# Softmax sums of the last four segments dealt one to each PE column tile, first memory queries put ahead of the others

## The chip, the cores and the metric

The kernel runs on one core of one Trainium2 chip. The metric is the time of one execution in device microseconds.

## The reference, cut to what matters

Four layers run one after the other: an FFT layer A, an attention layer B, A again, B again. Layer B cuts 2048 rows into 64 segments of 32. Each segment attends to 8 memory rows and to itself, for 32 heads of 128:

```python
for s in range(n_seg):
    h = jnp.concatenate([mem, xs], axis=1)            # 8 memory rows, 32 rows
    ...
    scores = jnp.where(mask, q @ k * scale, -1e9)
    p = _softmax(scores, axis=-1)                     # sum over keys, then divide
    o = p @ v ... Wo
    mem = o[:, :M, :]                                 # memory of the next segment
```

The kernel does all segments of a head at once. It works with one memory query per segment; only the first segment keeps the seven others, since its memory rows differ. These seven are "the first memory queries" (`PRE = 7`). A head thus has 64 x 33 + 7 = 2119 queries, in five groups: four of 15 segments and one of the last 4.

## The kernel before: the parts that matter

Keys lie on partitions in 17 tiles of 128. For every tile and group, the queries that see keys of that tile form a run of columns, and each run is one matmul in three stages: scores, sums, values. The layout puts the seven queries last, so they fall into the fifth group although their keys are in tile 0:

```python
    PRE = MEM - 1; SW = SEG + 1; GS = 15; NG = 5; NT = 17
    QPRE = NSEG * SW                   # the 7 first memory queries come last
    GQ = GS * SW                       # 495 columns per group
    def qbase(self, s):
        return self.SW * s
    # ... self.tiles[t] = [(group, lo, hi, offset in P), ...]
```

The sums are matmuls with a block of ones, 32 output rows wide. Four groups go to the four column tiles of the PE array (rows 0 to 31, 32 to 63 and so on of one PSUM buffer) and run side by side. The fifth goes to rows 0 to 31 of the last scores' buffer, that is to column tile 0, where the first group already is:

```python
def sums(h, P, ps_last):
    psl = pa.tile([128, 512], FP32, name="psl", tag="psl", bufs=1)
    ps4 = ps_last[0:32, 512 - NL:512]
    for i in range(max(len(r) for r in runs)):
        for g_ in range(NG):
            # ...
            dst = psl[32 * g_:32 * g_ + 32, :] if g_ < 4 else ps4
            nc.tensor.matmul(dst[:, lo - q0:hi - q0], lhsT=ones[:, 0:32], rhs=P[:, off:off + hi - lo], ...)
    # ... five ACT copies into sums_sb: 4 groups side by side, then 139 columns of the fifth
def sums_ln(h):    # Ln on ACT, sum into an accumulator on POOL
def sums_back(h):  # Exp(-x) on ACT = 1/sum, two stores to DRAM, one broadcast load to all partitions
def value_group(h, P, Rb, oT, g_):
    # matmuls of V with P into pso, then DVE multiplies pso by the reciprocals
```

All engines but POOL follow one manual order. In the pass of head h, keys, queries and values of h are computed, with scores and sums of h - 1 and values of h - 2 put in between:

```python
post = [lambda: sums(...), lambda: sums_ln(h - 1), lambda: sums_back(h - 1)]
merge(dense, parts + [g1[0], post[0], g1[1], post[1], g1[2], post[2], g1[3], g1[4]])
```

Of the kernel before, what the change touches and what calls it, by code (L numbers as in the profile page):

```python
# [691 lines left out]
class _Stream:  # L692
# [11 lines left out]
    NT = 17  # L704
    NK = NT * 128
    NQ = PRE + NSEG * SW
    QPRE = NSEG * SW
    GQ = GS * SW
    NM = PRE + NSEG
    NC = PRE + NSEG - 1  # L710
    NX = NSEG * SEG
# [3 lines left out]
    def __init__(self):  # L715
        PRE, SW, GS = self.PRE, self.SW, self.GS
        kseg = np.full(self.NK, -1)
        kpos = np.zeros(self.NK, dtype=int)
        kw = np.zeros(self.NK)
        kseg[0:PRE], kpos[0:PRE], kw[0:PRE] = 0, np.arange(PRE), 1  # L720
        for s in range(NSEG):
            b = self.kbase(s)
            rows = np.arange(b, b + SW)
            if s == NSEG - 1:
                rows[SW - self.TAIL:] = self.TAILK + np.arange(self.TAIL)
            kseg[rows] = s
            kpos[rows] = np.concatenate([[MEM - 1], MEM + np.arange(SEG)])
            kw[rows] = 1
            kw[b] = 1 if s == 0 else MEM
        qseg = np.zeros(self.NQ, dtype=int)  # L730
        qpos = np.zeros(self.NQ, dtype=int)
        qpos[self.QPRE:] = np.arange(PRE)
        for s in range(NSEG):
            b = self.qbase(s)
            qseg[b:b + SW] = s
            qpos[b:b + SW] = np.concatenate([MEM + np.arange(SEG), [MEM - 1]])
        self.hgap = [(self.hcol(a), self.hcol(b)) for a, b in ((502, 512), (1007, 1024), (1519, 1536), (2035, 2048))]
        self.q0 = [0] + [self.qbase(g * GS) for g in range(1, self.NG)] + [self.NQ]
        ok = (kseg[:, None] == qseg[None, :]) & ((qpos[None, :] < MEM) | (qpos[None, :] >= kpos[:, None]))
        full = np.where(ok, kw[:, None], 0.0)  # L740
        self.tiles = []
        cols = []
        off = 0
        for t in range(self.NT):
            blk = full[t * 128:(t + 1) * 128]
            used = np.flatnonzero(blk.any(axis=0))
            runs = []
            for g in range(self.NG):
                u = used[(used >= self.q0[g]) & (used < self.q0[g + 1])]
                if len(u):  # L750
                    lo, hi = int(u[0]), int(u[-1]) + 1
                    runs.append((g, lo, hi, off))
                    cols.append(blk[:, lo:hi])
                    off += hi - lo
            self.tiles.append(runs)
        self.NP = off
        self.mask = np.concatenate(cols, axis=1).astype(np.float32)
        self.parts = [[t] if t == self.NT - 1 else [t, t + 1] for t in range(0, self.NT, 2)]
        for p in self.parts:
            assert sum(hi - lo for t in p for _, lo, hi, _ in self.tiles[t]) <= 512  # L760
# [3 lines left out]
        return 512 * g + (self.PRE if g == 0 else 0) + self.SW * i  # L764

    def qbase(self, s):
        return self.SW * s

    def hcol(self, k):

# [268 lines left out]
def _b_fast_pass(tc, g, bs, env, flag_col, nxt=None):  # L1039
# [2 lines left out]
    hT, gq, oTm = bs.hT, bs.gq, bs.oTm  # L1042
    ones = g["ones"]
    oTx_d = g["oTx_d"]
    PRE, SW, GS, NG, NT, NQ, QPRE = st.PRE, st.SW, st.GS, st.NG, st.NT, st.NQ, st.QPRE
    scale = float(DH) ** -0.5
    Wd = {n: g[n].rearrange("(c p) h e -> p c (h e)", p=128) for n in ("Wq", "Wk", "Wv")}
    kruns = [(0, 502), (512, 1007), (1024, 1519), (1536, 2035), (2048, 2176)]
# [3 lines left out]
    pa = octx.enter_context(tc.tile_pool(name="b_pa", bufs=2, space=PSUM))  # L1052
    last = {}
    ar = env["ar"]
    GQ, NL = st.GQ, NQ - st.GQ * (NG - 1)
    HPRE, HL = H - 4, H - 2
    s6 = bs.s6
    s3, s4, s5 = (ar.get(s, f"b{bs.lname}") for s in ("S3", "S4", "S5"))
    Vs = [s3.bf(NT, 256) for _ in range(2)]
    s3.o = SLOT["S3"] - 4 * (GQ + NL)  # L1060
    accR, accS = s3.f32(GQ + NL), s3.f32(GQ + NL)
    wts = [{n: s6.bf(5, 256) for n in ("Wq", "Wk", "Wv")} for _ in range(2)]
    oTs = [s6.bf(st.NX) for _ in range(2)]
    QTs = [s4.bf(NQ + 1) for _ in range(2)]
    KTs = [s4.bf(st.NK) for _ in range(2)]
    Ps = [s5.bf(st.NP) for _ in range(2)]
    Es = [s5.bf(512) for _ in range(2)]
    Rb1, sums_sb = s5.f32(NQ), s5.f32(GQ + NL)
    Rs = [s4.f32(GQ + NL), g["R"][:]]
    if True:  # L1070
        nc.gpsimd.memset(sums_sb[:, GQ:], 1.0)
        for KT in KTs:
            for a, b in ((502, 512), (1007, 1024), (1519, 1536), (2035, 2048)):
                nc.gpsimd.memset(KT[:, a:b], 0.0)
# [40 lines left out]
        def q_m(w, h):  # L1115
            QT = QTs[h % 2]
            ps = pj.tile([128, 512], FP32, name="psq", tag="pj")
            chain(w["Wq"], h % 2, ps[:, 0:PRE], hT, 0, PRE)
            chain(w["Wq"], h % 2, ps[:, PRE:st.NM], gq, 0, NSEG)
            nc.scalar.mul(out=QT[:, QPRE:NQ], in_=ps[:, 0:PRE], mul=scale)  # L1120
            nc.scalar.mul(out=x_view(QT, 0, NSEG)[:, :, SEG], in_=ps[:, PRE:st.NM], mul=scale)

        def q_run(w, h, g_):
            QT = QTs[h % 2]
            lo, hi = kruns[g_]
            ps = pj.tile([128, 512], FP32, name="psq", tag="pj")
            chain(w["Wq"], h % 2, ps[:, 0:hi - lo], hT, lo, hi)
            n = GS if g_ < NG - 1 else 3
            o = st.kbase(g_ * GS) - lo
            qv = x_view(QT, st.qbase(g_ * GS), n)  # L1130
            nc.scalar.mul(out=qv[:, :, 0:SEG], in_=x_view(ps, o, n)[:, :, 1:SW], mul=scale)  # L1131
            if g_ < NG - 1:
                nc.scalar.mul(out=qv[:, :, SEG], in_=x_view(ps, o, n)[:, :, 0], mul=scale)
            if g_ == 0:
                nc.scalar.mul(out=QT[:, QPRE:NQ], in_=ps[:, 0:PRE], mul=scale)
            elif g_ == NG - 2:
                q_tail(QT, ps, SEG - st.TAIL, st.TAILK - lo, st.TAIL)
            elif g_ == NG - 1:
                nc.scalar.mul(out=x_view(QT, st.qbase(NSEG - 4), 4)[:, :, SEG], in_=ps[:, 0:3 * SW + 1:SW], mul=scale)
                q_tail(QT, ps, 0, 3 * SW + 1, SEG - st.TAIL)  # L1140
# [30 lines left out]

        def sums(h, P, ps_last):
            psl = pa.tile([128, 512], FP32, name="psl", tag="psl", bufs=1)
            ps4 = ps_last[0:32, 512 - NL:512]
            for i in range(max(len(r) for r in runs)):
                for g_ in range(NG):
                    if i >= len(runs[g_]):
                        continue
                    t, (_, lo, hi, off) = runs[g_][i]
                    dst = psl[32 * g_:32 * g_ + 32, :] if g_ < 4 else ps4  # L1180
                    nc.tensor.matmul(dst[:, lo - st.q0[g_]:hi - st.q0[g_]], lhsT=ones[:, 0:32], rhs=P[:, off:off + hi - lo],  # L1181
                                     start=(i == 0), stop=(i == len(runs[g_]) - 1), skip_group_check=True)
            for dst, src, ns in ((sums_sb[:, 0:GQ], psl, GS), (sums_sb[0:32, GQ:GQ + NL], ps4, NSEG - (NG - 1) * GS)):
                v, nx = x_view(src, 0, ns), ns * SEG
                nc.scalar.copy(out=dst[:, 0:nx].rearrange("p (r s j) -> p r s j", r=16, j=2), in_=byclass(v))
                nc.scalar.copy(out=dst[:, nx:nx + ns], in_=v[:, :, SEG])
            nc.scalar.copy(out=sums_sb[0:32, GQ + QPRE - 4 * GQ:GQ + NL], in_=ps4[:, QPRE - 4 * GQ:NL])  # L1187

        def sums_ln(h):
            nc.scalar.activation(out=Rs[h % 2], in_=sums_sb, func=ACTF.Ln, bias=g["floor"][:, 0:1])  # L1190
# [13 lines left out]
        def sums_back(h):  # L1204
            R = Rs[h % 2]
            nc.scalar.activation(out=R, in_=R, func=ACTF.Exp, scale=-1.0)
            if h == H - 1:
                return
            Rd = g["dram"].tile([1, NQ], FP32, name="Rd", tag="Rd", bufs=3)
            nc.sync.dma_start(out=Rd[0:1, 0:4 * GQ].rearrange("o (g n) -> (o g) n", g=4), in_=R[0:128:32, 0:GQ])  # L1210
            nc.sync.dma_start(out=Rd[0:1, 4 * GQ:NQ], in_=R[0:1, GQ:GQ + NL])
            nc.sync.dma_start(out=Rbs2[h % 2], in_=Rd[0:1, :].to_broadcast([128, NQ]))

        def sums_wide(P, Rb, g_):
            q0, n = st.q0[g_], st.q0[g_ + 1] - st.q0[g_]
# [7 lines left out]
        def value_group(h, P, Rb, oT, g_):  # L1223
# [4 lines left out]
                nc.tensor.matmul(pso[:, lo - q0:hi - q0], lhsT=V[:, t, (h % 2) * 128:(h % 2 + 1) * 128], rhs=P[:, off:off + hi - lo],  # L1228
                                 start=(i == 0), stop=(i == len(runs[g_]) - 1), skip_group_check=True)
            s0, ns = g_ * GS, min(GS, NSEG - g_ * GS)  # L1230
            po, nx = x_view(pso, 0, ns), ns * SEG
            if h < H - 1:
                rx, rm = Rb[:, q0:q0 + nx].rearrange("p (r s j) -> p r s j", r=16, j=2), Rb[:, q0 + nx:q0 + nx + ns]
            else:
                rq = x_view(Rb, q0, ns)
                rx, rm = byclass(rq), rq[:, :, SEG]
            nc.vector.tensor_tensor(out=oT.rearrange("p (r s j) -> p r s j", r=16, j=2)[:, :, s0:s0 + ns, :], in0=byclass(po), in1=rx, op=ALU.mult)  # L1237
            nc.vector.tensor_tensor(out=oTm[:, h, PRE + s0:PRE + s0 + ns], in0=po[:, :, SEG], in1=rm, op=ALU.mult)  # L1238
            if g_ < NG - 1:
                return  # L1240
            nc.vector.tensor_tensor(out=oTm[:, h, 0:PRE], in0=pso[:, QPRE - q0:n], in1=Rb[:, QPRE:NQ], op=ALU.mult)

        def store(h, oT):
            if h < HL:
# [39 lines left out]
        if True:  # L1284
            for h in range(H + 2):
# [7 lines left out]
                if h == 0:  # L1293
# [2 lines left out]
                    q_x(w, 1)  # L1296
                    s1 = ar.get("S1", f"b{bs.lname}")
                    oT0 = s1.bf(HL, 512)
                    Rbs2 = [s1.f32(NQ), Rb1]
                dense, parts, groups = [], [], []  # L1300
                if h < H:
                    def both(run):
# [51 lines left out]
    with octx:  # L1354
# [3 lines left out]
                          lambda c: [(PRE, st.NC, gq[:, c, 1:NSEG]), (0, PRE, gq[:, c, 1:2].to_broadcast([128, PRE]))], st.NM, st.NC)  # L1358
        xns = None
        if nxt is not None:  # L1360
            s3.o = SLOT["S3"] - 4 * (GQ + NL)
            xns = [s3.bf(D) for _ in range(3)]
            nxt.x = x
            nxt.begin_stage1(T)

# [218 lines left out]
def make_globals(ctx, tc, Wq, Wk, Wv, Wo, mem0):  # L1584
# [20 lines left out]
    g["st"] = st = _Stream()  # L1605
    g["gq"] = sp.tile([128, 5, NSEG], BF16, name="gqf")
    g["oTm"] = sp.tile([128, H, st.NM + 1], BF16, name="oTmf")
    g["R"] = sp.tile([128, st.GQ + st.NQ - st.GQ * (st.NG - 1)], FP32, name="R")
    g["m0"] = sp.tile([MEM, D], BF16, name="m0")
    g["u"] = sp.tile([128, 5, NSEG], BF16, name="u")  # L1610
    g["mask"] = sp.tile([128, st.NP], BF16, name="maskf")
# [110 lines left out]
```

## Time and profile before

| | before |
|---|---|
| median of 4 runs | 1580.68 us (1579.67 to 1581.49) |
| span of the profiled run | 1577.2 us |
| PE, ACT, DVE, POOL busy | 1541.9, 834.3, 783.7, 279.3 us |
| one block of sums, first start to what follows | 457 ns, x64 |
| stage B1, B2 (see below) | 667.44, 662.52 us |

The span, from the first instruction to the last, is some 2 us shorter than the time of the same run (1577.2 and 1579.07 us here). A "stage" is measured between two matmul starts in the trace: B1 from the first key matmul of layer 1's attention to the first transform matmul (line 424) of the FFT layer after it, B2 from the first key matmul of the second attention layer to the last matmul of the kernel. The lines that carry the bound are shown in the prediction. The page's rows of matmuls give the time that one spends in the pipe (165 to 375 ns each); what one costs is the distance to the next start.

### The profile page before, as it was taken

The page shows a single profiled execution, that of the slowest core. Times are in us where ns is not written, and L with a number is a line of the kernel's source. Part 1 is how long each engine was busy: PE and PEld are TensorE (multiplying, and loading weights), DVE is VectorE, ACT ScalarE, POOL GpSimd, SP SyncE. Part 2 cuts the span into 40 slices and gives each one's busy share as a digit, 9 for nine tenths or more (in the row PEclk, how much of TensorE's full clock was granted, in tenths as well). Part 3 has the DMA queues.
Part 4 walks back from the last instruction along what each step waited for, and adds up shares of the span by engine and source line. Part 5 has one row for each costly group of instructions (what it writes and reads, how often), then busy time and mean ns, then how long its engine had stood idle before and what let it go on. Part 6 is the DMA issues. An engine that isn't in the chain of part 4 may idle for free. (4 is left out here: it accounts for less than half of the span.)

```text
span 1577.2 us, 36639 instructions
## 1 busy us (share of the span) xinstructions
PE 1541.9 (98%) x14420; PEld 1073.3 (68%) x14421; DVE 783.7 (50%) x2198; ACT 834.3 (53%) x2549; POOL 279.3 (18%) x327
## 2 busy tenths in 40 slices
PE   6999999999999999999999999999999999999998
PEld 5676676666766666677766766666766666677775
DVE  7872545454554545533377545454555545543101
ACT  4584666666666666511126656666666666663000
POOL 3620121111212111100034111111212111120000
PEclk9999999999999999999999999999999999999999
DMA  4680545445454453745114515445454454437242
GB/s 170 213 305 6 153 129 141 130 121 175 122 149 122 134 163 104 216 103 172 51 55 148 182 54 143 128 122 175 124 147 122 136 160 130 142 97 227 68 130 62
DMA packets 159890, 214.13 MB, mean 136 GB/s; under 512 B 7198, under 2 KB 133468, under 8 KB 151772
## 3 DMA queue, kind: packets, MB, share of 16 engines
q1 hardware_dynamic: 159132, 209.41, 44.8%
q8 instruction: 114, 1.87, 0.5%
q0 software_dynamic: 576, 2.30, 0.4%
q14 instruction: 68, 0.56, 0.1%
HBM read 166.59 MB, written 45.09 MB: 134 GB/s over the span
## 5 line engine op out<-in xcount | busy, mean ns | idle before, releaser
L1087 PEld LDWEIGHTS <-bB_S 128*128 128x128 bf16 x3180 | 258.0, 97 | 174.7 <-issue 1.1
L1237 DVE TENSOR_TENSOR bB_S<-pso,bB_S 128x480 bf16<-128x480 f32 (+1 forms) x320 | 189.4, 592 | 246.7 <-PE pso L1228 235.6
L1166 ACT ACTIVATE bB_S<-pss 128x269 bf16<-128x269 f32 (+5 forms) x576 | 203.9, 386 | 199.1 <-PE pss L1163 194.0
L1393 PE MATMUL psx<-Wo_sb,bB_S 128*128 128x320 bf16 x2048 | 287.7, 299 | 0.0
L1146 DVE CAST bB_S<-psk 128x495 bf16<-128x495 f32 (+3 forms) x320 | 191.6, 599 | 114.2 <-PE psk L1087 75.8
L1393 PEld LDWEIGHTS <-bB_S 128*128 128x128 bf16 x2048 | 197.1, 98 | 74.3 <-DVE bB_S L1237 0.7
L1167 DVE TENSOR_TENSOR bB_S<-bB_S,maskf 128x269 bf16<-128x269 bf16 (+5 forms) x576 | 159.3, 288 | 162.1 <-ACT bB_S L1166 162.1
L1192 POOL TENSOR_TENSOR bB_S<-bB_S,bB_S 128x634 f32<-128x634 f32 x62 | 95.1, 1533 | 682.1 <-ACT bB_S L1187 682.1
L1155 ACT CAST bB_S<-psv 128x512 bf16<-128x512 f32 (+1 forms) x288 | 161.2, 560 | 75.7 <-PE psv L1153 75.1
L1131 ACT ACTIVATE bB_S<-psq 128x96 bf16<-128x96 f32 x300 | 152.3, 508 | 91.2 <-PE psq L1087 90.3
L1153 PE MATMUL psv<-bB_S,B2hT_S 128*128 128x256 bf16 x1360 | 166.2, 273 | 0.0
L1153 PE MATMUL psv<-bB_S,B1hT_S 128*128 128x256 bf16 x1360 | 166.2, 273 | 0.0
L1087 PE MATMUL psk<-B1hT_S,bB_S 128*128 128x495 bf16 (+3 forms) x800 | 162.4, 343 | 0.4 <-ACT bB_S L1108 0.2
L1087 PE MATMUL psk<-B2hT_S,bB_S 128*128 128x495 bf16 (+3 forms) x800 | 162.4, 343 | 0.3 <-ACT bB_S L1108 0.2
L1163 PEld LDWEIGHTS <-bB_S 128*128 128x128 bf16 x1216 | 99.6, 97 | 84.4
L1087 PE MATMUL psq<-B2hT_S,bB_S 128*128 128x495 bf16 (+5 forms) x780 | 153.2, 336 | 0.0
L1087 PE MATMUL psq<-B1hT_S,bB_S 128*128 128x495 bf16 (+5 forms) x780 | 153.2, 336 | 0.0
L1153 PEld LDWEIGHTS <-B1hT_S 128*128 128x128 bf16 x1360 | 127.5, 98 | 14.6 <-issue 0.2
L1153 PEld LDWEIGHTS <-B2hT_S 128*128 128x128 bf16 x1360 | 127.5, 98 | 14.6 <-issue 0.2
L1163 PE MATMUL pss<-bB_S 128*128 128x132 bf16 (+8 forms) x1216 | 133.0, 215 | 0.1
L1228 PE MATMUL pso<-bB_S,bB_S 128*128 128x132 bf16 (+8 forms) x1216 | 120.2, 216 | 1.6 <-DVE oTmf L1238 1.4
L1228 PEld LDWEIGHTS <-bB_S 128*128 128x128 bf16 x1216 | 90.6, 98 | 22.8 <-DVE oTmf L1238 4.0
(282 smaller groups left out, 1539.4 us busy)
## 6 DMA issues: line engine op xcount, KB each, us to landing
bB_S<-Rd SPq DMA_DIRECT2D x62, 1059.5 KB
oTx_d<-bB_S SPq DMA_DIRECT2D x60, 512.0 KB
bB_S<-oTx_d SPq DMA_DIRECT2D x46, 512.0 KB
bB_S<-in_B_Wq_dram SPq DMA_DIRECT2D x32, 320.0 KB
bB_S<-in_B_Wk_dram SPq DMA_DIRECT2D x32, 320.0 KB
bB_S<-in_B_Wv_dram SPq DMA_DIRECT2D x32, 320.0 KB
Wo_sb<-in_B_Wo_dram SPq DMA_DIRECT2D x4, 1280.0 KB
B1wv_S<-in_B_Wv_dram SPq DMA_DIRECT2D x10, 512.0 KB
```

The costliest lines, as they stand in the source:

```text
L1087: nc.tensor.matmul(ps, lhsT=w[:, ch, hh * 128:(hh + 1) * 128], rhs=src[:, ch, lo:hi], start=(ch == 0), stop=(ch == 4))
L1131: nc.scalar.mul(out=qv[:, :, 0:SEG], in_=x_view(ps, o, n)[:, :, 1:SW], mul=scale)
L1146: nc.vector.tensor_copy(out=KTs[h % 2][:, lo:hi], in_=ps[:, 0:hi - lo])
L1153: nc.tensor.matmul(ps[:, i * 256:(i + 1) * 256], lhsT=hT[:, ch, st.hcol((t + i) * 128):st.hcol((t + i) * 128) + 128], rhs=w["Wv"][:, ch, : ...
L1155: nc.scalar.copy(out=V[:, t:t + n, :].rearrange("p a b -> p (a b)"), in_=ps[:, 0:n * 256])
L1163: nc.tensor.matmul(ps[:, off - o0:off - o0 + hi - lo], lhsT=KT[:, t * 128:(t + 1) * 128], rhs=QT[:, lo:hi], start=True, stop=True)
L1166: nc.scalar.activation(out=E[:, 0:n], in_=ps[:, 0:n], func=ACTF.Exp)
L1167: nc.vector.tensor_tensor(out=P[:, o0:o0 + n], in0=E[:, 0:n], in1=bs.mask[:, o0:o0 + n], op=ALU.mult)
L1192: nc.gpsimd.tensor_tensor(out=accS, in0=accS, in1=sums_sb, op=ALU.add)
L1228: nc.tensor.matmul(pso[:, lo - q0:hi - q0], lhsT=V[:, t, (h % 2) * 128:(h % 2 + 1) * 128], rhs=P[:, off:off + hi - lo], start=(i == 0), st ...
L1237: nc.vector.tensor_tensor(out=oT.rearrange("p (r s j) -> p r s j", r=16, j=2)[:, :, s0:s0 + ns, :], in0=byclass(po), in1=rx, op=ALU.mult)
L1393: self.tc.nc.tensor.matmul(ps[:, 0:320], lhsT=lhs(h, k // 2), rhs=self.g["Wo_sb"][:, h, c0:c0 + 320], start=(h == 0), stop=(h == H - 1))
```

## The change

The intent: take three small matmuls per head away (the seven queries join tile 0's first run in scores, values and sums), and give the fifth group's sums to all four column tiles, 33 columns each, rather than to the one that has most already. The rows of sums become 535 columns wide and not 634, so Ln, Exp, the accumulators and the stores get shorter, and one of two stores goes. The next layer's norm rows move from the buffer that also holds the accumulators to another. The core of the diff, with cuts marked:

```diff
-    QPRE = NSEG * SW
+    NR = GQ + SW + PRE
...
     def qbase(self, s):
-        return self.SW * s
+        return self.PRE + self.SW * s
...
         def sums(h, P, ps_last):
-            ps4 = ps_last[0:32, 512 - NL:512]
-            for i in range(max(len(r) for r in runs)):
-                for g_ in range(NG):
-                    dst = psl[32 * g_:32 * g_ + 32, :] if g_ < 4 else ps4
...
+            for i in range(max(len(r) for r in runs[:-1])):
+                for g_ in range(NG - 1):
+                    ...  # as before, into psl on tile g_
+            top = ps_last[:, 512 - SW:512]
+            for g_ in range(NG - 1):
+                jobs.append((g_, top, off + SW * g_, True, g_ < NG - 2))
+            jobs.append((NG - 2, top[:, SW - (tail[2] - tail[1]):SW], tail[3], False, True))
...
-            nc.sync.dma_start(out=Rd[0:1, 0:4 * GQ].rearrange(...), in_=R[0:128:32, 0:GQ])
-            nc.sync.dma_start(out=Rd[0:1, 4 * GQ:NQ], in_=R[0:1, GQ:GQ + NL])
+            nc.sync.dma_start(out=Rd[0:1, :].rearrange("o (g n) -> (o g) n", g=4), in_=R[0:128:32, :])
...
-            s3.o = SLOT["S3"] - 4 * (GQ + NL)
-            xns = [s3.bf(D) for _ in range(3)]
+            xns = [s1.bf(D) for _ in range(3)]
```

The last job is a run of 5 columns: the last segment has four keys in tile 15, so its sums need one more matmul, on tile 3.

More of the change, by code (lines that the diff above doesn't have):

```diff
@@ L731, in __init__ @@
         qpos = np.zeros(self.NQ, dtype=int)
-        qpos[self.QPRE:] = np.arange(PRE)
+        qpos[0:PRE] = np.arange(PRE)
         for s in range(NSEG):
@@ L1044, in _b_fast_pass @@
     oTx_d = g["oTx_d"]
-    PRE, SW, GS, NG, NT, NQ, QPRE = st.PRE, st.SW, st.GS, st.NG, st.NT, st.NQ, st.QPRE
+    PRE, SW, GS, NG, NT, NQ, NR = st.PRE, st.SW, st.GS, st.NG, st.NT, st.NQ, st.NR
     scale = float(DH) ** -0.5
@@ L1054, in _b_fast_pass @@
     ar = env["ar"]
-    GQ, NL = st.GQ, NQ - st.GQ * (NG - 1)
     HPRE, HL = H - 4, H - 2
@@ L1059, in _b_fast_pass @@
     Vs = [s3.bf(NT, 256) for _ in range(2)]
-    s3.o = SLOT["S3"] - 4 * (GQ + NL)
-    accR, accS = s3.f32(GQ + NL), s3.f32(GQ + NL)
+    s3.o = SLOT["S3"] - 4 * NR
+    accR, accS = s3.f32(NR), s3.f32(NR)
     wts = [{n: s6.bf(5, 256) for n in ("Wq", "Wk", "Wv")} for _ in range(2)]
@@ L1067, in _b_fast_pass @@
     Es = [s5.bf(512) for _ in range(2)]
-    Rb1, sums_sb = s5.f32(NQ), s5.f32(GQ + NL)
-    Rs = [s4.f32(GQ + NL), g["R"][:]]
+    Rb1, sums_sb = s5.f32(4 * NR), s5.f32(NR)
+    Rs = [s4.f32(NR), g["R"][:]]
     if True:
-        nc.gpsimd.memset(sums_sb[:, GQ:], 1.0)
+        nc.gpsimd.memset(sums_sb[:, GS * SW + SW:], 1.0)
         for KT in KTs:
@@ L1119, in q_m @@
             chain(w["Wq"], h % 2, ps[:, PRE:st.NM], gq, 0, NSEG)
-            nc.scalar.mul(out=QT[:, QPRE:NQ], in_=ps[:, 0:PRE], mul=scale)
-            nc.scalar.mul(out=x_view(QT, 0, NSEG)[:, :, SEG], in_=ps[:, PRE:st.NM], mul=scale)
+            nc.scalar.mul(out=QT[:, 0:PRE], in_=ps[:, 0:PRE], mul=scale)
+            nc.scalar.mul(out=x_view(QT, PRE, NSEG)[:, :, SEG], in_=ps[:, PRE:st.NM], mul=scale)
         def q_run(w, h, g_):
@@ L1134, in q_run @@
             if g_ == 0:
-                nc.scalar.mul(out=QT[:, QPRE:NQ], in_=ps[:, 0:PRE], mul=scale)
+                nc.scalar.mul(out=QT[:, 0:PRE], in_=ps[:, 0:PRE], mul=scale)
             elif g_ == NG - 2:
@@ L1173, in sums @@
             psl = pa.tile([128, 512], FP32, name="psl", tag="psl", bufs=1)
-            ps4 = ps_last[0:32, 512 - NL:512]
-            for i in range(max(len(r) for r in runs)):
-                for g_ in range(NG):
-                    if i >= len(runs[g_]):
-                        continue
-                    t, (_, lo, hi, off) = runs[g_][i]
-                    dst = psl[32 * g_:32 * g_ + 32, :] if g_ < 4 else ps4
-                    nc.tensor.matmul(dst[:, lo - st.q0[g_]:hi - st.q0[g_]], lhsT=ones[:, 0:32], rhs=P[:, off:off + hi - lo],
-                                     start=(i == 0), stop=(i == len(runs[g_]) - 1), skip_group_check=True)
@@ L1183, in sums @@
-            for dst, src, ns in ((sums_sb[:, 0:GQ], psl, GS), (sums_sb[0:32, GQ:GQ + NL], ps4, NSEG - (NG - 1) * GS)):
-                v, nx = x_view(src, 0, ns), ns * SEG
-                nc.scalar.copy(out=dst[:, 0:nx].rearrange("p (r s j) -> p r s j", r=16, j=2), in_=byclass(v))
-                nc.scalar.copy(out=dst[:, nx:nx + ns], in_=v[:, :, SEG])
-            nc.scalar.copy(out=sums_sb[0:32, GQ + QPRE - 4 * GQ:GQ + NL], in_=ps4[:, QPRE - 4 * GQ:NL])
+            jobs = []
+            for i in range(max(len(r) for r in runs[:-1])):
+                for g_ in range(NG - 1):
+                    t, (_, lo, hi, off) = runs[g_][i]
+                    b = lo - st.q0[g_] + (PRE if g_ else 0)
+                    jobs.append((g_, psl[:, b:b + hi - lo], off, i == 0, i == len(runs[g_]) - 1))
@@ new lines, in sums @@
+            tail, (_, lo, hi, off) = runs[-1][0][1], runs[-1][1][1]
+            top = ps_last[:, 512 - SW:512]
+            for g_ in range(NG - 1):
+                jobs.append((g_, top, off + SW * g_, True, g_ < NG - 2))
+            jobs.append((NG - 2, top[:, SW - (tail[2] - tail[1]):SW], tail[3], False, True))
+            for g_, dst, off, first_, last_ in jobs:
+                nc.tensor.matmul(dst[32 * g_:32 * g_ + 32, :], lhsT=ones[:, 0:32], rhs=P[:, off:off + dst.shape[1]], start=first_, stop=last_,
+                                 skip_group_check=True)
@@ L1189, in sums_ln @@
+            v, nx = x_view(psl, PRE, GS), GS * SEG
+            nc.scalar.copy(out=sums_sb[:, 0:nx].rearrange("p (r s j) -> p r s j", r=16, j=2), in_=byclass(v))
+            nc.scalar.copy(out=sums_sb[:, nx:nx + GS], in_=v[:, :, SEG])
+            nc.scalar.copy(out=sums_sb[0:32, NR - PRE:NR], in_=psl[0:32, 0:PRE])
+            nc.scalar.copy(out=sums_sb[:, NR - PRE - SW:NR - PRE], in_=top)
         def sums_ln(h):
@@ L1208, in sums_back @@
                 return
-            Rd = g["dram"].tile([1, NQ], FP32, name="Rd", tag="Rd", bufs=3)
-            nc.sync.dma_start(out=Rd[0:1, 0:4 * GQ].rearrange("o (g n) -> (o g) n", g=4), in_=R[0:128:32, 0:GQ])
-            nc.sync.dma_start(out=Rd[0:1, 4 * GQ:NQ], in_=R[0:1, GQ:GQ + NL])
-            nc.sync.dma_start(out=Rbs2[h % 2], in_=Rd[0:1, :].to_broadcast([128, NQ]))
+            Rd = g["dram"].tile([1, 4 * NR], FP32, name="Rd", tag="Rd", bufs=3)
+            nc.sync.dma_start(out=Rd[0:1, :].rearrange("o (g n) -> (o g) n", g=4), in_=R[0:128:32, :])
+            nc.sync.dma_start(out=Rbs2[h % 2], in_=Rd[0:1, :].to_broadcast([128, 4 * NR]))
         def sums_wide(P, Rb, g_):
@@ L1230, in value_group @@
             s0, ns = g_ * GS, min(GS, NSEG - g_ * GS)
-            po, nx = x_view(pso, 0, ns), ns * SEG
-            if h < H - 1:
-                rx, rm = Rb[:, q0:q0 + nx].rearrange("p (r s j) -> p r s j", r=16, j=2), Rb[:, q0 + nx:q0 + nx + ns]
+            o, nx = PRE if g_ == 0 else 0, GS * SEG
+            po = x_view(pso, o, ns)
+            if h == H - 1:
+                rq = x_view(Rb, q0 + o, ns)
+                rx, rm, rp = byclass(rq), rq[:, :, SEG], Rb[:, 0:PRE]
+            elif g_ < NG - 1:
+                r = Rb[:, NR * g_:NR * g_ + NR]
+                rx, rm, rp = r[:, 0:nx].rearrange("p (r s j) -> p r s j", r=16, j=2), r[:, nx:nx + GS], r[:, NR - PRE:NR]
             else:
-                rq = x_view(Rb, q0, ns)
+                rq = Rb.rearrange("p (s n) -> p s n", n=NR)[:, :, NR - PRE - SW:NR - PRE]
                 rx, rm = byclass(rq), rq[:, :, SEG]
@@ L1238, in value_group @@
             nc.vector.tensor_tensor(out=oTm[:, h, PRE + s0:PRE + s0 + ns], in0=po[:, :, SEG], in1=rm, op=ALU.mult)
-            if g_ < NG - 1:
-                return
-            nc.vector.tensor_tensor(out=oTm[:, h, 0:PRE], in0=pso[:, QPRE - q0:n], in1=Rb[:, QPRE:NQ], op=ALU.mult)
+            if g_ == 0:
+                nc.vector.tensor_tensor(out=oTm[:, h, 0:PRE], in0=pso[:, 0:PRE], in1=rp, op=ALU.mult)
         def store(h, oT):
@@ L1298, in _b_fast_pass @@
                     oT0 = s1.bf(HL, 512)
-                    Rbs2 = [s1.f32(NQ), Rb1]
+                    Rbs2 = [s1.f32(4 * NR), Rb1]
                 dense, parts, groups = [], [], []
@@ L1360, in _b_fast_pass @@
         if nxt is not None:
-            s3.o = SLOT["S3"] - 4 * (GQ + NL)
-            xns = [s3.bf(D) for _ in range(3)]
+            xns = [s1.bf(D) for _ in range(3)]
             nxt.x = x
@@ L1607, in make_globals @@
     g["oTm"] = sp.tile([128, H, st.NM + 1], BF16, name="oTmf")
-    g["R"] = sp.tile([128, st.GQ + st.NQ - st.GQ * (st.NG - 1)], FP32, name="R")
+    g["R"] = sp.tile([128, st.NR], FP32, name="R")
     g["m0"] = sp.tile([MEM, D], BF16, name="m0")
```

## The prediction

> **What bounds the kernel now.** I read four views of the kernel before, in this order: the page's busy table, the chain of waits that ended last, PE's own waits, and the timeline of PE in windows of under a microsecond. The busy table:
>
> ```profile
> PE 1541.9 (98%) x14420; PEld 1073.3 (68%) x14421; DVE 783.7 (50%) x2198; ACT 834.3 (53%) x2549; POOL 279.3 (18%) x327
> ...
> PEclk9999999999999999999999999999999999999999
> ```
>
> PE is near full and always at full clock, the others are at half. A busy PE row does not prove much, because matmuls overlap, so I asked who is waited for. The chain runs nearly everywhere from one matmul to the next:
>
> ```profile
> PE psv L1153 9%; PE psk L1087 9%; PE psx L1393 9%; PE psq L1087 9%; PE pso L1228 2%; PE pss L1163 2%; PE psl L1181 1%; PE psq L1106 1%; PE psm L863 0%; PE psvb L1486 0%; PE psg L1554 0%; DMA Rd<-bB_S 0%; PE pss L1181 0%; ACT bB_S L1108 0%; PE psw L1218 0%
> ```
>
> and PE's waits in the part that the change touches (lines 1163, 1181, 1228) come to 1.4 us in all:
>
> ```profile
> PE ps L324 <- DVE A1xn_S L315: 10.0, 1, 10.0
> PE pso L1228 <- DVE oTmf L1238: 1.4, 4, 0.5
> ```
>
> In the windows 150 to 650 us and 924 to 1430 us (the two attention stages) PE is busy 499.83 of 500.00 and 505.18 of 506.00 us. So the kernel is a queue of matmuls. The time changes by what the change takes from PE's issue order, and hardly by anything else.
>
> The mean of a matmul row (170 ns for 7 columns) is how long one is in the pipe, not what it costs. The cost is the distance from its start to the next start. Three narrow windows of the timeline give it:
>
> ```profile
> 400.66 0.43 PE L1163 MATMUL pss<-bB_S 128*128 128x132 bf16 x5
> 400.92 0.37 PE L1087 MATMUL psk<-B1hT_S,bB_S 128*128 128x495 bf16 x1
> ```
>
> ```profile
> 414.70 0.27 PE L1228 MATMUL pso<-bB_S,bB_S 128*128 128x7 bf16 x3
> 414.81 0.66 PE L1087 MATMUL psk<-B1hT_S,bB_S 128*128 128x128 bf16 x6
> ```
>
> ```profile
> 408.98 0.80 PE L1087 MATMUL psq<-B1hT_S,bB_S 128*128 128x499 bf16 x3
> 409.71 0.24 PE L1181 MATMUL psl<-bB_S,ones 128*32 128x132 bf16 x4
> 409.77 0.17 PE L1181 MATMUL pss<-bB_S,ones 128*32 128x7 bf16 x1
> 409.78 0.30 PE L1181 MATMUL psl<-bB_S,ones 128*32 128x137 bf16 x7
> 409.87 0.17 PE L1181 MATMUL pss<-bB_S,ones 128*32 128x5 bf16 x1
> 409.89 0.24 PE L1181 MATMUL psl<-bB_S,ones 128*32 128x148 bf16 x4
> 409.96 0.22 PE L1181 MATMUL pss<-bB_S,ones 128*32 128x132 bf16 x1
> 410.01 0.22 PE L1181 MATMUL psl<-bB_S,ones 128*32 128x119 bf16 x1
> 410.16 0.36 PE L1228 MATMUL pso<-bB_S,bB_S 128*128 128x132 bf16 x3
> ```
>
> The first shows five score matmuls (132, 7, 144, 148, 119 columns) in 0.26 us. The second shows the last value group (7, 5, 132 columns) in 0.11 us. The third shows one block of sums: 19 matmuls of 32 output rows each, 0.45 us from the first to what follows it, with four of them starting within 10 ns and so running side by side. From the start times of all 64 occurrences in the trace I take medians: 7 columns cost 28 ns in the score stage and 28 in the value stage, 5 columns 25 to 27, 132 columns 57 to 58, 144 columns 62, 148 columns 63. One block of sums takes 457 ns (455 to 460 in all 64).
>
> **What the Trainium skill says.** TensorE: Matmul & The Clock Gate, Back-to-back issue gap, gives an isolated gap of N/2.4 + 2.5 ns and a floor of about 25 ns for up to 64 columns. The trace agrees: 132 columns at 57 to 58 ns (formula 57.5), 7 columns at 28 ns. So a 7-column matmul nearly costs the floor, and widening a neighbour by 7 columns costs 7/2.4 = 3 ns. TensorEngine Tiling (Array Packing), Key Properties, says that tiles run independently and that "Mode switching requires drain". The trace agrees with both: the four starts 3 ns apart, and around a block of sums the gap is 97 ns longer than the columns before it going in, 99 ns coming out. The same page, PSUM Bottleneck, warns that PSUM eviction may become the limit; here ACT, which evicts the sums, is 53% busy and PE waits for it nowhere in these stages.
>
> **The change part by part.** There are 32 heads in each of two layers, so each per-head item counts 64 times. The order of instructions in the changed kernel, set against the old, confirms the counts.
>
> 1. Scores. The seven memory queries now lie ahead of segment 0, so tile 0 is one matmul of 139 columns in place of 132 and 7. Removed 28 ns, added 3 ns: 25 ns x 64 = **1.6 us**, all on PE's path.
> 2. Values. The 7-column matmul of the last group joins the first matmul of the first group in the same way: 25 ns x 64 = **1.6 us**.
> 3. Sums. In the old block, column tile 0 had to do the first group and the whole last group: 132, 7, 144, 5, 148, 132, 119 columns, starting at 0, 68, 98, 160, 186, 250 and 308 ns. Then 50 ns of columns and 99 ns of leaving make 457. The other three tiles had their last start at 199 to 208 ns and sat idle. The new block deals the 132 columns out as 33 to each tile: tile 0 does 139, 144, 148, 119, 33; tile 3, now the longest, does 132, 137, 141, 112, 33, 5. From the old starts of tile 3 (10, 78, 142, 208) its 33 should start near 260 (112 columns cost 51), its 5 near 289 (33 columns cost the floor, 27 to 29), and the block should end between 289 + 99 = 388 and 289 + 25 + 99 = 413. I take 400: 57 ns x 64 = **3.6 us**. Two matmuls are added per block, which cancels the two removed in 1 and 2, so the count stays the same to within two; the gain is in where they run.
> 4. Off the path. ACT copies per block go from five (581 + 215 + 263 + 163 + 169 ns) to four: the 263 and the 163 go, one of 128x33 comes at some 230 (estimate, from the 215 of 15 columns): 0.2 us. Ln and Exp fall from 634 to 535 columns, some 0.1 us each by their own slope (estimate, 828 x 99/634 is the upper bound, 0.13). So ACT falls by some 0.4 us x 64 = 25 us of 834. POOL's adds fall from 1533 ns to about 1533 x 535/634 = 1294, that is 124 x 0.24 = 30 us. One of two small stores per head goes (62), and the broadcast that follows grows by 1% (2140 columns for 2119). DVE has the same 2198 instructions, with the 7-column multiply (156 ns) moved from the last group to the first. All this is hidden, since PE does not wait for it: worth 0.
> 5. The next layer's norm rows in another buffer. In the hand-over after layer 1 (650 to 740 us) PE is busy 89.22 of 90 us, so nothing is there to win: 0.
>
> Sum: 1.6 + 1.6 + 3.6 = 6.8 us, and 1580.4 - 6.8 = 1573.6 us, or 0.4%.
>
> **The rivals.** (a) The sums gain nothing, because the block is held by the drain or by loading the ones into the array (21 loads in place of 19), not by tile 0's queue. For it: 196 of the 457 + 97 ns around a block are drain. Against it: tile 0's starts follow its columns one by one. Then only 3.2 us come: 1577. (b) The whole block shortens further, because all four tiles' queues are better filled and the start lag of 7 to 35 ns between rounds goes. If the block took the bare columns (583 on tile 0, 243 ns) plus 99, it would gain 115 ns x 64 = 7.4 us, together 10.6: 1570. (c) A new wait. The sums of the last four segments now need all 128 rows of the last scores' buffer, one DVE operation of 156 ns is added to the first value group, and each layer's end has DVE behind: there PE waits 0.65 and 0.40 us. That could cost 0.3 us per layer, not more. (d) Start addresses of the queries shift by 7 columns, so odd and even change places. Matmuls of 132 to 148 columns cost 1 to 7 ns over their columns, without a pattern that I could tie to the address; if there is one, 34 matmuls per head x 64 x 1 ns = 2.2 us either way. (e) The single store of 4x535 delays the broadcast. Its wait now touches PE once, for 0.3 us, at each layer's start.
>
> **Range and chances.** The centre is 1573.6. Rival (a) and a loss from (d) give 1577 to 1579, rival (b) with a gain from (d) gives 1568. Runs of the old kernel spread by 1.3 us. I choose 1569 to 1578. A gain over 2% would need 31 us, four times what lies on these three lines; a loss of 2% would need a wait that no view hints at.
>
> **What would show it.** Right: the 7-column rows of lines 1163 and 1228 gone, and 139-column ones spaced near 60 ns; a block of sums near 400 ns from first start to what follows; entry and exit gaps still 97 and 99; ACT near 809 and POOL near 249 us busy, the span unmoved by them; PE still over 499 of 500 us busy in the attention windows. Wrong: a block of sums at 450 or at 340; a new line in PE's waits that names ACT, DVE or the store; or all score and value matmuls slower by a few ns each.

## More of the kernel before

Runs of one kernel scatter by 1 to 3 us, so where a difference is smaller than that I read it from start times in the trace and not from the clock. There is one trace of each kernel.

## The result, and the profile after

The changed kernel takes 1571.99 us (median of 4 runs, 1571.49 to 1573.32) against 1580.68. The ratio is 0.9947, with a 95% interval of 0.9929 to 0.9964. The same kernel once more, in a later job (the run e10_again), gave 1572.91 us and 0.9950 (0.9936 to 0.9964). All outputs are right.

The busy table of the kernel after, in the same columns as before (busy us, share of the span, instructions):

```profile
PE 1536.3 (98%) x14418; PEld 1072.5 (68%) x14419; DVE 787.4 (50%) x2198; ACT 818.5 (52%) x2485; POOL 228.5 (15%) x327
```

PE has two instructions fewer and is as full as before: still the bound. The three narrow windows of its timeline that answer to those in the prediction (start us, length us, engine, line, operation, count) are, for scores:

```profile
399.30 0.41 PE L1162 MATMUL pss<-bB_S 128*128 128x139 bf16 x4
399.54 1.00 PE L1086 MATMUL psk<-B1hT_S,bB_S 128*128 128x495 bf16 x4
```

for the last value group:

```profile
413.25 0.25 PE L1231 MATMUL pso<-bB_S,bB_S 128*128 128x5 bf16 x2
413.34 0.87 PE L1086 MATMUL psk<-B1hT_S,bB_S 128*128 128x128 bf16 x7
```

and for one block of sums:

```profile
408.33 0.42 PE L1185 MATMUL psl<-bB_S,ones 128*32 128x139 bf16 x16
408.58 0.20 PE L1185 MATMUL pss<-bB_S,ones 128*32 128x33 bf16 x5
408.72 0.41 PE L1231 MATMUL pso<-bB_S,bB_S 128*128 128x132 bf16 x4
```

Four score matmuls take 0.24 us where five took 0.26, two value matmuls 0.09 where three took 0.11, and 21 sums take 0.39 us where 19 took 0.45. Where the time went is seen when the distances from each matmul's start to the next are added up by kind over the whole trace:

| us | before | after | difference |
|---|---|---|---|
| scores | 68.0 | 66.8 | -1.2 |
| values | 70.6 | 69.6 | -1.0 |
| sums, without the way in | 29.2 | 24.7 | -4.6 |
| keys | 288.1 | 287.8 | -0.2 |
| queries, V, output products | 291.3, 297.0, 279.8 | 291.3, 297.1, 279.9 | +0.2 |
| stage B1 | 667.44 | 664.04 | -3.40 |
| stage B2 | 662.52 | 659.12 | -3.40 |

"The way in" is what the matmul ahead of a block of sums costs beyond its usual distance (499 columns: 305 ns for 211). It is the same in both kernels and left out of all rows.

The two attention stages give 6.80 us. The two profiled spans differ by 7.4 us, so 0.6 us more lie outside the stages. Two larger things happen there, and neither is an effect that the change aimed at.

First, the end. From the start of the last matmul to the end of the span it is 7.05 us before and 6.13 after, 0.9 us less. Second, the clock. Of the twelve traces, nine have a stretch of 3.4 us at half clock that starts 71 to 75 us into the span, inside the first FFT layer; in these the time from the first matmul to the first key matmul is 123.7 to 125.0 us. The three without it (before, e2_first_only, e5_tile3_first) take 122.8. The windows view shows it (window, its length, then busy us of PE, PEld, DVE, ACT, POOL, and the granted clock; the clock is the last but two). Before:

```profile
70.00:76.00 6.00, 3.76 (x28) 2.67 (x29) 4.75 (x8) 3.50 (x12) 2.17 (x2) 1.00 0.64 219
```

After:

```profile
70.00:76.00 6.00, 4.46 (x26) 3.20 (x26) 4.01 (x7) 2.81 (x9) 1.76 (x2) 0.72 0.58 198
```

A second stretch, at 843 to 853 us, is in all twelve traces. The one at 71 us is in the changed kernel's trace and not in the one before, and works against the change by about 1 us. It does not go with the change: e5_tile3_first differs from the changed kernel in the order of a few sums and has none, and e3_rows_only, with the sums of before, has one. The rest is small: the time before the first matmul is 0.5 us shorter (10.04 to 9.55), the FFT layer between the stages 0.1. Together -0.9 + 0.95 - 0.5 - 0.1 = -0.6 us.

### The profile page after: what moved, and what is told of

Same layout as the page of the kernel before. It is cut to its first block, busy times and chain, and to the rows that moved or that the text cites. A ratio compares the mean times of both kernels' runs of the same rounds, so it can differ in the third digit from the quotient of the medians.

```text
span 1569.8 us, 36492 instructions
## 1 busy us (share of the span) xinstructions
PE 1536.3 (98%) x14418; PEld 1072.5 (68%) x14419; DVE 787.4 (50%) x2198; ACT 818.5 (52%) x2485; POOL 228.5 (15%) x327
## 5 line engine op out<-in xcount | busy, mean ns | idle before, releaser
L1245 DVE TENSOR_TENSOR bB_S<-pso,bB_S 128x480 bf16<-128x480 f32 (+1 forms) x320 | 194.2, 607 | 237.3 <-PE pso L1231 226.5
L1196 POOL TENSOR_TENSOR bB_S<-bB_S,bB_S 128x535 f32<-128x535 f32 x62 | 69.9, 1128 | 726.8 <-ACT bB_S L1191 713.9
```

The costliest lines, as they stand in the source:

```text
L1196: nc.gpsimd.tensor_tensor(out=accS, in0=accS, in1=sums_sb, op=ALU.add)
L1245: nc.vector.tensor_tensor(out=oT.rearrange("p (r s j) -> p r s j", r=16, j=2)[:, :, s0:s0 + ns, :], in0=byclass(po), in1=rx, op=ALU.mult)
```

## The experiments

Theory: PE's issue order is the whole of it. A block of sums lasts as long as the longest queue among the four column tiles, then the array drains; a small matmul costs some 25 ns of its own queue. Rivals: the block is set by the number of matmuls or by the drain; the two parts pay only together; the gain comes from a shorter ACT, from the store, or from the norm rows. Ten kernels were run, one of them the changed kernel again. Runs of before beside them had medians of 1580.61 (e1 to e4), 1580.65 (e5 to e8) and 1581.04 us (e9, e10).

**e1_deal_only**: the deal alone. The changed kernel with the seven queries put last again, so that they are a run of their own in scores and values and a job of 7 columns on tile 0 in the sums.

```diff
-        return self.PRE + self.SW * s
+        return self.SW * s
+                if i == 0:
+                    jobs.append((0, psl[:, 0:PRE], runs[-1][0][1][3], False, False))
```

> Only the last four segments are dealt out, one to each column tile; the memory queries stay last. Theory (the block of sums lasts as long as its longest tile queue, then a drain): tile 0 does 132, 7, 144, 148, 119, 33, tile 3 does 132, 137, 141, 112, 33, 5, both end near 286 to 290 ns, so the block is 380 to 395 ns as in the changed kernel (384), 62 to 77 ns under the 457 of before; the rows of 7 columns stay in scores and values. Time 4 to 5 us under before: 1575 to 1577. Rival (the gain needs fewer small matmuls on tile 0, the deal alone gives nothing): block over 430 ns, time within 2 us of before.

It took 1575.84 us, ratio 0.9959 (0.9946 to 0.9973). The block is 395 ns in the median, and the stages are 665.24 and 660.34 us, 4.38 us under before. The deal pays alone. The block is 11 ns over the changed kernel's: with the extra 7 columns tile 0 is again the longest, its last 33 columns start at 283 ns, where in the changed kernel they start near 260. (The trace does not name a matmul's tile. In the changed kernel 33 columns start at 251, 256, 260 and 262 ns; tile 0's 119 columns before them start at 207 and cost some 50, so only the last two can be tile 0's.)

**e2_first_only**: the seven queries first alone. The kernel before with the new query order, the fifth group still on tile 0.

```diff
-        return self.SW * s
+        return self.PRE + self.SW * s
-            ps4 = ps_last[0:32, 512 - NL:512]
+            ps4 = ps_last[0:32, 512 - (NL - PRE):512]
```

> Only the memory queries go first; all four last segments stay on column tile 0 (139, 144, 5, 148, 132, 119). Theory: scores and values lose 1.2 and 1.0 us as in the changed kernel, the block of sums falls by the 7-column matmul alone, from 457 to 425 to 432 ns (1.6 to 2.0 us): 3.5 to 4.5 us under before, 1576 to 1577. Rival (the two parts only pay together): under 2 us, block still over 445 ns.

It took 1576.25 us, ratio 0.9969 (0.9956 to 0.9983). The block is 434 ns, just above the range expected; scores and values lost 1.1 and 1.0 us; the stages are 665.80 and 660.88, 3.28 us under before. So e1 and e2 give 4.38 + 3.28 = 7.66 us apart and 6.80 together. The difference is the 7-column matmul in the sums: it costs 23 ns (457 - 434) while tile 0 is the longest queue, and 11 ns (395 - 384) once the others are as long. (23 - 11) x 64 = 0.8 us.

**e3_rows_only**: the norm rows alone, on the kernel before.

```diff
-            s3.o = SLOT["S3"] - 4 * (GQ + NL)
-            xns = [s3.bf(D) for _ in range(3)]
+            xns = [s1.bf(D) for _ in range(3)]
```

> Only the next layer's norm rows move to the other buffer. Theory: PE is busy 89 of 90 us in that hand-over, so 0: within 1 us of before (1579.7 to 1581.5), sums, scores and values to the ns as before. Rival (the rows waited for POOL's accumulators, and this is the 2 us that the matmul starts of the changed kernel leave unexplained): 1.5 to 2.5 us under before.

It took 1580.09 us, ratio 0.9998 (0.9984 to 1.0011); the stages are 667.46 and 662.52 us, as before to 0.02. This part is worth nothing in time.

**e4_split**: what a switch of the array's mode costs. The changed kernel with its sums cut in two, the first value group in between; no matmul more or less.

```diff
-                    merge(dense, parts + [g1[0], post[0], ...
+                    merge(dense, parts + [lambda: (early(), g1[0]()), post[0], ...
```

> The changed kernel with its block of sums cut in two, the first value group between the halves: same matmuls, one more entry into and exit from the 32-column mode per head and layer. Theory (the mode switch costs a fixed 94 ns going in and 85 to 100 coming out): 62 split blocks x 180 to 200 ns = 11 to 12.5 us more than the changed kernel: 1583 to 1584.5, so slower than before. Rival (what looks like a drain is the wait for the last probabilities or for the block's own results): the early half pays little, under 4 us more.

It took 1586.99 us, slower than before: ratio 1.0036 (1.0021 to 1.0052). The stages are 670.86 and 665.94 us, 13.6 us over the changed kernel's, which is 220 ns for each of the 62 splits. In the timeline of this kernel the two halves are

```profile
412.63 0.31 PE L1179 MATMUL psl<-bB_S,ones 128*32 128x139 bf16 x8
412.87 0.42 PE L1242 MATMUL pso<-bB_S,bB_S 128*128 128x139 bf16 x4
413.13 1.22 PE L1086 MATMUL psq<-B1hT_S,bB_S 128*128 128x499 bf16 x5
414.28 0.30 PE L1196 MATMUL psl<-bB_S,ones 128*32 128x148 bf16 x8
414.40 0.20 PE L1196 MATMUL pss<-bB_S,ones 128*32 128x33 bf16 x5
414.54 0.41 PE L1242 MATMUL pso<-bB_S,bB_S 128*128 128x132 bf16 x4
```

0.24 and 0.26 us, together 0.50 where one block took 0.38, and the way in is paid twice (5.8 us more in all, 62 x 94 ns). The early half has no late data to wait for, as DVE wrote the last of its probabilities about 1 us earlier, and pays all the same: the cost goes with entering and leaving the 32-column mode. I had expected 180 to 200 ns. Each half has its own longest queue, which by the starts makes some 10 ns of the rest; what is left of it is not traced.

**e5_tile3_first**: the four tiles in the order 3, 2, 1, 0 in each round.

```diff
-                for g_ in range(NG - 1):
+                for g_ in range(NG - 2, -1, -1):
```

> The changed kernel with the four tiles issued in the order 3, 2, 1, 0 in each round of the sums, so that tile 3, whose queue has one matmul more, starts first and not 10 ns late. Theory (longest queue): the block falls by 7 to 10 ns, from 384 to 374 to 378, worth 0.4 to 0.7 us, too little for the clock to show: 1571 to 1572.5. Rival (the order of issue does not matter, or the last issued sets the end): block 384 or more.

It took 1572.43 us, ratio 0.9952 (0.9938 to 0.9965), the same as the changed kernel; the block is 383 ns, not 374 to 378. A miss. Tile 3's last start did come earlier, at 276 ns and not 286, but tile 0, now 10 ns later, starts its last 33 columns at 272 (near 260 before), and the exit from the last start grew from 98 to 107 ns. With some 14 ns for 33 columns and 2 for 5 (estimate, from the 211 ns of 499 columns), tile 0 now ends last, at 286 ns against 278 on tile 3; in the changed kernel tile 3 ended last, at 289 against some 275. So this order hands the longest queue to the other tile and wins 1 ns. An order with both ahead of tiles 1 and 2 was not run. No version that I ran beats the changed kernel.

**e6_more_on_012** and **e7_more_on_3**: three more 5-column matmuls at the end of each block, into columns that nobody reads; in e6 one on each of tiles 0, 1 and 2, in e7 all three on tile 3.

```diff
+            jobs += [(g_, psl[:, 505:510], tail[3], False, True) for g_ in range(NG - 2)]     # e6
+            jobs += [(NG - 2, psl[:, 505:510], tail[3], False, True) for _ in range(3)]       # e7
```

> The changed kernel with one more 5-column matmul on each of tiles 0, 1 and 2 at the end of the block, into columns that nobody reads (result stays right): 24 matmuls in place of 21. Theory (longest queue): they run beside tile 3's last one, the block grows by no more than the 3 to 12 ns of their issue. Rival (the block is set by the number of matmuls or weight loads): 24/21 of 384, or 3 x 25 = 75 ns more.

> The changed kernel with the same three extra 5-column matmuls, but all on tile 3. Theory (longest queue, 25 ns for each small matmul in one queue): the block grows by 72 to 80 ns, from 384 to some 460; 64 x 75 ns = 4.8 us on the span. Rival (count of matmuls alone): the same growth as with the three on tiles 0, 1 and 2.

The block is 387 ns in e6 (+3) and 461 ns in e7 (+77), with 24 matmuls in both. Lines of e6, then of e7:

```profile
410.04 0.42 PE L1186 MATMUL psl<-bB_S,ones 128*32 128x139 bf16 x16
410.29 0.19 PE L1186 MATMUL pss<-bB_S,ones 128*32 128x33 bf16 x4
410.32 0.17 PE L1186 MATMUL psl<-bB_S,ones 128*32 128x5 bf16 x3
410.33 0.17 PE L1186 MATMUL pss<-bB_S,ones 128*32 128x5 bf16 x1
410.43 0.41 PE L1232 MATMUL pso<-bB_S,bB_S 128*128 128x132 bf16 x4
```

```profile
409.83 0.42 PE L1186 MATMUL psl<-bB_S,ones 128*32 128x139 bf16 x16
410.08 0.20 PE L1186 MATMUL pss<-bB_S,ones 128*32 128x33 bf16 x5
410.15 0.22 PE L1186 MATMUL psl<-bB_S,ones 128*32 128x5 bf16 x3
410.29 0.41 PE L1232 MATMUL pso<-bB_S,bB_S 128*128 128x132 bf16 x4
```

From the first line to the last of each it is 0.39 and 0.46 us. The stages of e7 are 4.7 us longer than the changed kernel's (666.41 and 661.48 us), as 64 x 77 ns = 4.9 asks. The same three matmuls are nearly free on the tiles that wait and cost 25 ns each on the one that does not: the longest queue decides, not the count. The single times (1575.25 and 1578.62 us) say less than these lines. In e6 the two attention stages are those of the changed kernel to 0.02 us, so what its span has more lies in the FFT layers.

**e8_act_double**: ACT's largest copy of the sums done twice.

```diff
             nc.scalar.copy(out=sums_sb[:, 0:nx].rearrange(...), in_=byclass(v))
+            nc.scalar.copy(out=sums_sb[:, 0:nx].rearrange(...), in_=byclass(v))
```

> The changed kernel with ACT's largest copy of the sums (128x480, 581 ns) done twice per head: 64 x 0.58 = 37 us more ACT work, more than the 16 us that the change took from ACT. Theory (ACT, POOL and the stores are hidden): the time stays within 1 us of the changed kernel, 1571 to 1573. Rival (part of the 8.7 us came from a shorter ACT, so from a shorter hold of the scores' buffer): 2 us or more slower than the changed kernel.

It took 1572.53 us, ratio 0.9955 (0.9939 to 0.9970). ACT is busier than in the kernel before (its busy table against 834.3 there):

```profile
PE 1536.8 (98%) x14418; PEld 1072.7 (68%) x14419; DVE 786.9 (50%) x2198; ACT 847.3 (54%) x2549; POOL 228.6 (15%) x327
```

and the stages are 664.19 and 659.25 us, 0.3 us over the changed kernel's in all. ACT's shorter work is hidden.

**e9_two_stores** and **e10_again**: the changed kernel with its store cut into 4x495 and 4x40, and the changed kernel itself beside it.

```diff
-            nc.sync.dma_start(out=Rd..., in_=R[0:128:32, :])
+            nc.sync.dma_start(out=Rv[:, 0:GQ], in_=R[0:128:32, 0:GQ])
+            nc.sync.dma_start(out=Rv[:, GQ:NR], in_=R[0:128:32, GQ:NR])
```

> The changed kernel with the one store of reciprocals per head cut into two again (4x495 and 4x40), so the 62 stores that the change removed are back. Theory (stores are hidden; the attention stages stay at 664.0 and 659.1 us from their first key matmul): the stages to within 0.3 us, time within 1.5 us of the changed kernel. Added guess: the end after the last matmul was 6.8 to 7.4 us in the three kernels with two stores per head and 6.1 to 6.5 in the seven with one, which looks like the place where the instruction stream ends; then it is 6.8 to 7.4 here. Rival (the store's shorter path is part of the gain): the stages 1 us or more longer.

> The changed kernel itself once more, beside the one with two stores on the same chip: its stages again 664.0 and 659.1 us, its end again 6.1 to 6.5 us, and whatever differs from the first profile lies in the first 125 us or at the moments of half clock. 1571 to 1573.5.

They took 1573.63 us (ratio 0.9953, 0.9939 to 0.9966) and 1572.91. e10 has stages of 664.09 and 659.10 us and an end of 6.21, as expected. e9 has stages of 664.49 and 659.50, 0.8 us more in all: more than the 0.3 that I had allowed for each, and less than the rival's 1 us. The place is one wait at each layer's start, where DVE holds a copy of the keys until the store of the first reciprocals has left the buffer that both share, and PE then waits for DVE. Lines of e9 (the bracket gives the idle time before and what ended it), then of the changed kernel:

```profile
158.42 0.28 PE L1162 MATMUL pss<-bB_S 128*128 128x132 bf16 x2
...
158.90 0.88 DVE L1145 CAST bB_S<-psk 128x128 bf16<-128x128 f32 x2 [6.50 <-DMA Rd<-bB_S]
...
159.24 1.00 PE L1086 MATMUL psk<-B1hT_S,bB_S 128*128 128x495 bf16 x4 [0.54 <-DVE bB_S L1145]
```

```profile
156.51 0.28 PE L1162 MATMUL pss<-bB_S 128*128 128x132 bf16 x2
156.90 1.21 PE L1086 MATMUL psk<-B1hT_S,bB_S 128*128 128x495 bf16 x5
```

The gap that PE has there over the matmul's own columns is 0.70 and 0.59 us in e9's two layers and 0.28 and 0.19 in the changed kernel. In the kernel before, whose second store was a small one (1x139), it is 0.33 and 0.26, so the change itself won only 0.1 us by it.

e9's end is 7.18 us. The four kernels with two stores per head have ends of 6.81 to 7.36 us, the eight with one have 6.08 to 6.50. So the 0.9 us at the end go with the 62 instructions on the sync queue. In the kernel before, two drains of the sync queue close to the end lie 0.86 us apart, after 0.06. In e9 they lie 0.20 us apart, and 0.7 us pass just ahead of them, so the gap is not tied to one instruction. What fills it no run here tests.

## Why the prediction was right, point by point

**The bound.** PE's order of issue, with nothing else in the way: right. The attention stages carry 6.80 us of the change, and e3 and e8 show that the norm rows and ACT's shorter work are worth nothing. Four readings on the way were loose. The chain reaches back only to some 884 us (its shares add up to 43%), so for the first attention layer the windows carry the argument alone. PE is not always at full clock: a digit 9 stands for 90% or more, and there is a stretch at half clock at 846 us. The 63 ns for 148 columns hold for scores; in values it is 69. And "four times what lies on these three lines" should read four times the gain: by start distances, the three lines hold some 170 us.

**Step 1, scores, 1.6 us.** Right mechanism, term too large: it is 1.2 us. I took 28 ns for the 7-column row and 3 for the wider neighbour, 25 per head. By means it is 18. The row's 28 go, but 132 to 139 columns costs 3 more, the 144 columns that followed go from 62 to 67, the 119 from 52 to 55 and the 148 by 1, so 16 stay; another 2 are the shorter gap at the layers' start (see e9). So the matmul behind the small one took 5 ns less than it takes without it; why, no run shows.

**Step 2, values, 1.6 us.** The same, 1.0 us or 16 ns per head by means: the row's 29 go, the 139, the 144 (63 to 67) and the 5 (25 to 29) cost 3 to 4 more each and the 148 one less, so 19 stay. 3 of these are given back at each layer's end, where the first value group has one DVE multiply more before its buffer is free: the longest gap on PE there grew from 0.65 to 0.75 us in both layers. e1, where that multiply stays in the last group, keeps the 0.65, and e2 has the 0.75. This was rival (c), below the 0.3 us per layer that I gave as its limit. PE's waits show it, before as in the prediction, and after as

```profile
PE pso L1231 <- DVE oTmf L1248: 1.2, 2, 0.6
PE pso L1231 <- DVE oTmf L1246: 0.5, 2, 0.2
```

where line 1248 is the 7-column multiply and the columns are us in total, times, longest. In all it is 1.7 us for 1.4, so by name it is the new wait on DVE that I had listed as a sign of being wrong, but with 0.3 us it does not touch the argument.

**Step 3, sums, 3.6 us.** The queue model was right, the size low: 4.6 us. The starts were within 3 ns (33 columns at 260 or 262 for 260, 5 columns at 286 for 289). I set the end between 388 and 413 ns and took the middle; it is 384, just below that range, as the way out ended 98 ns after the last start, without the 25 ns floor of the small matmul added.

**Step 4, off the path, 0.** Right. Added up by row, ACT's sums, Ln and Exp fell by 24.9 us as estimated (25); the busy table fell only 15.8, to 818.5 and not 809, since small copies overlap there. POOL's adds fell further than I had worked out, to 1128 ns and not 1294 (228.5 us busy, not 249). Not foreseen were the 0.1 us at the layers' start and the 0.9 us at the end that went with the store.

**Step 5, 0.** Right (e3).

**Sum.** 6.8 us, as measured between the matmul starts, but partly by luck: one term 1.0 us too small against two that were 0.4 and 0.6 too large. The medians differ by 8.7 us; the end explains 0.9 of the rest, and what remains is within the scatter of the runs and the moments of half clock.

**The rivals.** (a), no gain in the sums, fell with e1. (b), the lag between rounds vanishing, fell with the starts, which still lie some 65 ns apart for 132 to 141 columns. (d), the shift of addresses by 7, shows nothing: the score and value matmuls of the second to fourth groups, whose columns did not change, have the same medians to within 2 ns. (e), a later broadcast, did not come: the gap at the layers' start fell from 0.33 and 0.26 us to 0.28 and 0.19.

## What to carry to other kernels

When matmuls share the array as column tiles, add up the columns of each tile and level them; three small matmuls more cost 3 ns on tiles that waited and 77 ns on the one that did not. Keep such work in one block, as each further entry into and exit from the mode cost 0.2 us here. Price a small matmul that you remove by what its neighbours do afterwards: 28 ns of distance were worth 16 to 19.

## What the Trainium skill lacked or had wrong

- TensorE: Matmul & The Clock Gate, The mechanism (in its Part 3), says that matmuls start in program order. Across column tiles the traces show otherwise: in the kernel before, the 144-column matmul of tile 0 precedes the three 137-column ones of the other tiles in the program and starts at 98 ns, they at 71 to 78. Within a tile order holds, as far as the starts tell the tiles apart.
- The same page, Measured speedup vs the span model, gives the span of one pack of equal tiles. It lacks the case of several rounds of unequal ones: there the block ended with the longest queue (387 against 461 ns for the same 24 matmuls).
- TensorEngine Tiling (Array Packing), Key Properties, says that a mode switch drains the array, without a size. Here the way in cost 94 to 97 ns over the columns before it, the way out ended 98 ns after the start of a 5-column matmul, and one more pair of switches, with its own queues, cost 220 ns.
- TensorE: Matmul & The Clock Gate, Back-to-back issue gap: the floor of about 25 ns for small matmuls agrees (25 to 28 ns). That the neighbours of a small matmul take 3 to 5 ns more each once it is gone is not there.
- GPSIMD Engine Reference, Elementwise — side-by-side cycle accounting, has one cost per element (some 2.6 cycles) for an add of two tensors. Here 99 columns fewer of 634 took 1533 to 1128 ns, 4.1 ns for each column taken away, more than the 2.4 ns that each column cost on average before (spans on POOL are rough in this profile); why, no run shows.
